# Pages of a folded weight: two single-page PSUM turns joined into one two-page turn

## The chip, the cores and the metric

The kernel runs on 1 core of one Trainium2 chip. The metric is the device time of one execution in microseconds; the number compared is the median of several executions. In 3 runs the kernel before took 734.44, 734.89 and 735.2 us, a median of 734.89 us.

## The reference, cut to what matters

An attention with 32 memory slots per head, followed by two feed-forward layers over all 2304 tokens:

```python
a = softmax(phi, axis=2)                       # over the sequence
k_m, v_m = a^T k, a^T v                        # per head: 32 x 64
attn = softmax(q @ k_m^T / 8)                  # per head: 576 x 32
x = (attn @ v_m) joined over the 8 heads       # 2304 x 512
x = relu(x @ w_in1)**2 @ w_out1                # layer 1, d_ff = 2048
h = x @ w_in2
out = (h * tanh(softplus(h))) @ w_out2         # layer 2
```

There are 4 batches, 8 heads, 576 tokens in a batch and a head size of 64. Everything is in 32-bit floats.

## The kernel before, in words

**What W' is.** The kernel never forms `attn @ v_m`. It folds the values into the first weight: for each batch b, W'_b = v_m(b) times w_in1, head by head, is 8 heads x 32 slots = 256 rows by 2048 columns, and layer 1 is then attn @ W'_b. W'_b is cut into 8 pages of 256 columns, named (b, j). To keep precision, a page holds a rounded high part and the low rest, and the product h (lines 713 to 715, `h_products`) takes three matmuls for each half of the 256 rows.

**A turn.** A page is made by 8 small matmuls (64 rows of the array, 32 columns of weights, 256 columns streamed) into the PSUM tile that `banks2` hands out: two banks, one buffer, tag "bb", shared with the attention scores and with the transposes of phi. ACT then copies the result to the high half of the page, and DVE subtracts the copy from the PSUM result to give the low half. Only then can the next user of "bb" start. `w_part` (line 580) does this for one page: matmuls at line 585, copy at 591, subtraction at 592. `w_pair` (line 605) does it for pages j and j + 1 of one batch: 16 matmuls at line 611, which put the first page into columns 0 to 255 and the second into columns 256 to 511 of both banks, and then the copies and subtractions of `take` (lines 618, 619) for the one and for the other. With `now=True` these are issued at once; otherwise they wait for the next step's `w_out`.

**The pages' places.** Pages live in a ring of 8 buffers (`page`, line 63); a new page takes the buffer of the one made eight earlier and waits for its last reader. The converted weights that the turns read, `wt["i1", j]`, lie in a ring of 4 buffers (line 229): page j + 4 of w_in1 can be written once both batches have used page j. The conversion `Conv` (from line 171) turns the raw 8-byte words into floats, one unit of 128 columns of w_in1 ("i1", u; page j is units 2j and 2j + 1) or one unit of w_out1 ("o1", u) for each `tick`: an ACT pass (line 204), two DVE passes (lines 234 and 240) and, for w_out1, a split (lines 223 and 263). `need(key, u)` ticks until that unit is done.

**The stages.** For batches 0 and 1, layer 1 goes in groups of d_ff blocks of 128: `GROUPS = [4, 6, 6]`, f = 0 to 3, 4 to 9, 10 to 15. The loop at line 1064 runs over 10 sub-tiles i. i = 0 to 3 are the first group, each on half a batch (288 tokens; i = 0 is written out by hand in `first_tile`). Then each of the other groups has three parts: part 0 is the first 344 tokens of batch 0, part 1 the remaining 232 of batch 0 with the first 232 of batch 1, part 2 the last 344 of batch 1 (i = 4 to 6 and i = 7 to 9). `a_tile` (line 724) runs one sub-tile: for each block fc it issues the product h, `tick(fc)`, relu and square, the split of the result g into high and low (lines 742 and 745), `mid(fc)`, the second product three blocks behind (`mm2_step`, lines 665 to 667, 12 matmuls), and last `post(fc)`, which is where the pages are made. The loads are SP's (sync) DMA queue's, issued by the conversion as its buffers come free.

**Where the pages are made before.** From `post` (line 1112): at i = 1, fc = 2 page (1,0) and fc = 3 page (1,1); at i = 3, fc = 2 page (0,2); at i = 4, fc = 4 page (0,3), fc = 6 page (0,4), fc = 8 page (1,2); at i = 5, fc = 4 the pair (1,3), (1,4); at i = 6, fc = 8 page (0,5); at i = 7, fc = 10 page (0,6), fc = 12 page (0,7), fc = 14 page (1,5); at i = 8, fc = 10 the pair (1,6), (1,7). The branch at lines 1114 to 1116 is never taken. Batches 2 and 3 get their pages in pairs.

**The order of the work.** The Python order is not the order on the chip: when the program is built, a scheduler with a timeline of its own puts each engine's instructions in order, and keeps to dependencies and to the explicit ones (`issue_after`, `written`). Matmuls of a page that nothing waits for yet can so land ahead of their place, or between others. Each engine then runs its own list strictly in that order.

After the ten sub-tiles, batches 2 and 3 follow as tiles of 288 tokens with all 16 blocks, beside the preparation of layer 2's weights (`Fold`), whose raw loads and stores share the DMA engines; then comes layer 2, whose order is fixed by hand.

Of the kernel before, what the change touches and what calls it, by code (L numbers as in the profile page):

```python
# [8 lines left out]
F32R = mybir.dt.float32r  # L9
# [7 lines left out]
B, H, S, D, M = 4, 8, 576, 64, 32  # L17
DM, FF = 512, 2048
P = 128
# [21 lines left out]
def body(tc, q, kvm, kvt, phi, w_in1, w_out1, w_in2, w_out2, out):  # L41
# [21 lines left out]
    def page(shape, dt, name):  # L63
        return PG.tile(shape, dt, tag="pg", name=name, bufs=NPG)
# [8 lines left out]
    for p in range(2):  # L73
        t = Y.tile([P, (NC + 1) * P], F32, name=f"phi{p}")
# [5 lines left out]
    def load_phi(b, p):  # L80
        nc.sync.dma_start(phi_t[p][:, at[p]:at[p] + S], phi[b, p])
# [14 lines left out]
    def load_q(b, half):  # L96

        q_t[b, half] = []
        for i in range(2):
            if b < 2 and half == 1:  # L100
                tag = f"wol{2 + i}" if b else f"wo{'hl'[i]}4"
                t = wo.tile([P, 2, T], F32, tag=tag, name=f"q{b}{half}{i}")
            else:
                t = Y.tile([P, 2, T], F32, tag="q", name=f"q{b}{half}{i}", bufs=2)
            nc.sync.dma_start(
                t.rearrange("p g t -> p (g t)"), q[b, half, :, 2 * i * T:2 * (i + 1) * T])
            q_t[b, half].append(t)
# [29 lines left out]
    wt = {}  # L137
# [15 lines left out]
    @contextlib.contextmanager  # L153
    def written(*engines):

        traced = nc.cur_bb.bb.instructions
        last = {x.engine: x for x in traced}
        seen = traced[-1]
        yield
        start = next(k for k in reversed(range(len(traced))) if traced[k] is seen) + 1  # L160
        for x in traced[start:]:
            if x.engine not in engines:
                continue
            if x.engine in last:
                tc.add_manual_dep(
                    x, last[x.engine].name,
                    mybir.DependencyInfo(mybir.DependencyClass.NoSync, mybir.DependencyReason.DATA),
                    reason="written")
            last[x.engine] = x
# [262 lines left out]
    def banks2(name):  # L432
        return psum2.tile([P, 2, 512], F32, tag="bb", name=name)

    rc_t, et_t, kk_t, kT, vT = {}, {}, {}, {}, {}
# [142 lines left out]
    wp = {}  # L578

    def w_part(b, j, lo, hi, split=False):  # L580

        ps = banks2(f"pw{b}{j}{lo}")[:, :, :hi - lo]
        for g in range(4):
            for p in range(2):
                nc.tensor.matmul(  # L585
                    ps[M * g:M * g + M, p], vT[b][D * p:D * p + D, M * g:M * g + M],
                    wt["i1", j][D * p:D * p + D, g, lo:hi], start=True, stop=True)
        if (b, j) not in wp:
            wp[b, j] = page([P, 2, 2, 256], F32R, f"wp{b}{j}")
        t = wp[b, j]  # L590
        nc.scalar.copy(t[:, 0, :, lo:hi], ps)
        rest = lambda: nc.vector.tensor_sub(t[:, 1, :, lo:hi], ps, t[:, 0, :, lo:hi].bitcast(F32))
        if split:
            return rest
        rest()
# [6 lines left out]
                f()  # L602
        wait_w.clear()

    def w_pair(b, j, now=False):

        ps = banks2(f"pw{b}{j}p")
        for i in range(2):
            for g in range(4):
                for p in range(2):  # L610
                    nc.tensor.matmul(
                        ps[M * g:M * g + M, p, 256 * i:256 * i + 256],
                        vT[b][D * p:D * p + D, M * g:M * g + M],
                        wt["i1", j + i][D * p:D * p + D, g], start=True, stop=True)

        def take(i):
            t = wp[b, j + i] = page([P, 2, 2, 256], F32R, f"wp{b}{j + i}")
            nc.scalar.copy(t[:, 0], ps[:, :, 256 * i:256 * i + 256])
            nc.vector.tensor_sub(t[:, 1], ps[:, :, 256 * i:256 * i + 256], t[:, 0].bitcast(F32))

        for i in range(2):
            if now:
                take(i)
            else:
                wait_w.append(lambda i=i: take(i))
# [25 lines left out]
    def drain(*lanes):  # L651
        while any(lanes):
            for lane in lanes:
                run_step(lane)
# [116 lines left out]
    def place(i):  # L771
        if i in deep:
# [3 lines left out]
    c1 = Conv(order, place,  # L776
              lambda key, u: key != "i1" or u < 8 or (1, u // 2 - 4) in wp)
# [257 lines left out]
    def attn_later(b, half):  # L1035
        def nxt():
            if b < 2:
                if (b, half) == (1, 0):
                    load_q(2, 0)
                return  # L1040
            nb, nh = (b, 1) if half == 0 else (b + 1, 0)
            if nb < B:
                load_q(nb, nh)
        return [[lazy(lambda: attn_unit(b, half, nxt)), 5 if b > 1 else 4]]
# [19 lines left out]
    for i, (f0, f1, segs) in enumerate(subs):  # L1064
        b, half, part = i // 2, i % 2, (i - 4) % 3 if i > 3 else None
        final = i == len(subs) - 1
        if i == 0:
            with written(mybir.EngineType.DVE, mybir.EngineType.Activation):
                first_tile()
            c1.hold = False  # L1070
            c1.store()
            c1.load(2 * GROUPS[0] - 3)
            continue
        elif i == 1:
            c1.limit, c1.after, c1.paced = 2 * GROUPS[0], "lo", True
            lanes, n_steps = [[iter(range(2)), 2]] + attn_later(1, 1), 1
        elif i == 2:
            c1.limit, c1.after = len(c1.order), (1, 0)
        elif i == 3:
            drain(lanes)  # L1080
            c1.after = (1, 1)
            load_q(2, 0)
            load_phi(2, 0)
            load_phi(2, 1)
            load_kv(2, 0)
            load_tail(2)
        elif i == 4:
            c1.after = None
        elif i == len(subs) - 2:
            lanes, n_steps = kv_later(2), 2  # L1090
        elif final:
            drain(lanes)
            lanes, n_steps = attn_later(2, 0), 2
            load_page(0)
            load_page(1)

        def tick(fc):
            if len(c1.done) < 2 * NF:
                c1.tick()
            else:  # L1100
                if not fold.loaded:
                    fold.load(3)
                if part and fc - f0 in (0, LAG + 1):
                    fold.tags = (("x", "at"), ("ys0", "x", "at"), ("ys0",), ("ys0", "ys1"))[
                        2 * part - 2 + (fc > f0)]
                if final or part == 1 and fc > f0:
                    fold.tick(pops=1)

        def mid(fc):
            run_step(lanes, n_steps)  # L1110

        def post(fc):
            if part is None:
                if half == 0 and fc % 2 == 0 and fc + 2 < f1 and i != 2:
                    c1.need("i1", fc + 3)
                    w_part(b, fc // 2 + 1, 0, 256)
                if i == 1 and fc + 1 == f1:
                    w_part(1, fc // 2, 0, 256)
                if half == 1 and fc + 2 == f1:
                    if b == 0:  # L1120
                        w_part(1, f0 // 2, 0, 256)
                    else:
                        c1.need("i1", f1 + 1)
                        w_part(0, f1 // 2, 0, 256)
            elif part == 0:
                if (fc - f0) % 2 == 0 and fc + 2 < f1:
                    c1.need("i1", fc + 3)
                    w_part(0, fc // 2 + 1, 0, 256)
                if fc >= f0 + 2:
                    c1.need("o1", fc - 2)  # L1130
                if fc + 1 == f1:
                    c1.need("o1", fc)
                if fc + 2 == f1:
                    w_part(1, f0 // 2, 0, 256)
            elif part == 1:
                if fc == f0:
                    w_pair(1, f0 // 2 + 1, True)
            elif fc + 2 == f1 and not final:
                c1.need("i1", f1 + 1)
                w_part(0, f1 // 2, 0, 256)  # L1140
            if final and fc - f0 in (1, 3):
                w_pair(2, fc - f0 - 1)
            if final and fc < f1 - 2:
                load_page(fc - f0 + 2)

        a_tile(segs, f0, f1, tick, mid, post, ("mm",) if i in (0, 1, 5) else ("mm", "b0"))
    drain(lanes)

# [8 lines left out]
    b, nb = 2, 3  # L1157
# [174 lines left out]
    now = 0  # L1332
# [139 lines left out]
    banks, tmp, g = {}, {}, {}  # L1472
# [4 lines left out]
    for now, (kind, i, one, two) in enumerate(plan):  # L1477
# [11 lines left out]
        if now + AHEAD < len(plan) and plan[now + AHEAD][0] == "b":  # L1489
            _, _, j, k = plan[now + AHEAD]  # L1490
# [73 lines left out]
```

## Time and profile before

| what | value |
|---|---|
| median of 3 runs | 734.89 us (734.44 to 735.2) |
| the profiled execution's own time | 734.3 us |
| its span, first to last instruction | 732.5 us |
| PE (matmuls) busy | 725.0 us, 99% |
| DVE busy | 523.5 us, 71% |
| ACT busy | 414.0 us, 57% |
| matmuls of single-page turns in the loop, line 585 | 10 turns x 16 records |
| matmuls of two-page turns, line 611 | 10 turns x 32 records |

The terms of the prediction are made against the profiled execution (734.3 us), which lies 0.59 us under the median. Each matmul of a fp32 turn shows as two records. In a timeline row the columns are the start in us, the length in us, the engine, the line, the operation, the output and inputs, the shape and the number of instructions merged into the row; in brackets stands how long the engine sat idle before it, and what ended that. Matmul lengths overlap: the time that one takes from PE is the distance between two starts.

### The profile page before, as it was taken

The numbers are of one execution on the slowest core, as the hardware profiler recorded it, in microseconds if no ns is written. First come the engines' busy times: TensorE is split into PE (matmuls) and PEld (weight loads), VectorE is DVE, ScalarE is ACT, GpSimd is POOL, SyncE is SP. The second block draws the span as 40 slices with busy tenths as digits, with TensorE's granted clock in tenths as the row PEclk, the third lists the DMA queues.
The fourth block names the chain that finished last, engine by engine and source line by source line (L and its number), as shares of the span: only waits on it lengthen the run. The fifth ranks groups of instructions, "written<-read, shape, count | busy, mean of one in ns | idle before, by whom it ended". The sixth has DMA issues, their size and how long they took to land.

```text
span 732.5 us, 15173 instructions
## 1 busy us (share of the span) xinstructions
PE 725.0 (99%) x5417; PEld 691.5 (94%) x5417; DVE 523.5 (71%) x1142; ACT 414.0 (57%) x937; POOL 62.0 (8%) x120
## 2 busy tenths in 40 slices
PE   8999999999999999999999999999999999999998
PEld 7788988998888899999999999999999999999997
DVE  5999766343887889899957769854658873556674
ACT  4869757553766698767644347532336551335552
POOL 0000000000122333243311000000000000000000
PEclk9999999999999999999999999999999999999999
DMA  9997542044689899878969998899988899888882
GB/s 337 400 407 280 178 136 92 30 159 151 229 303 377 305 316 339 287 274 312 330 230 358 392 315 250 271 298 305 307 251 249 253 293 297 250 252 249 254 272 77
DMA packets 88011, 195.26 MB, mean 267 GB/s; under 512 B 10112, under 2 KB 21376, under 8 KB 87936
## 3 DMA queue, kind: packets, MB, share of 16 engines
q1 hardware_dynamic: 78976, 164.92, 67.7%
q0 software_dynamic: 8960, 29.37, 10.3%
q8 instruction: 43, 0.70, 0.4%
q14 instruction: 32, 0.26, 0.1%
HBM read 151.26 MB, written 42.99 MB: 265 GB/s over the span
## 4 chain that ended last, share of the span: by engine, by line
PE 91%; DMA 4%; DVE 2%; ACT 2%; issue 1%; SPq 0%; DVEq 0%; ACTq 0%
PE a L667 8%; PE a L665 8%; PE a L666 8%; PE hb L1361 8%; PE hb L1363 8%; PE hb L1362 8%; PE h L713 5%; PE h L714 4%; PE h L715 4%; DMA raw_i<-in_moe_w_in_dram 2%; PE pw L585 1%; PE fill L789 1%; PE b22acc L1447 1%; PE b12acc L1445 1%; PE b02acc L1447 1%; PE b22acc L1445 1%
## 5 line engine op out<-in xcount | busy, mean ns | idle before, releaser
L665 PE MATMUL a<-g,o1h 128*128 128x288 f32 (+2 forms) x464 | 140.2, 311 | 1.3 <-ACT g L742 1.3
L666 PE MATMUL a<-g,o1l 128*128 128x288 f32 (+2 forms) x464 | 140.8, 309 | 0.0
L667 PE MATMUL a<-g,o1h 128*128 128x288 f32 (+2 forms) x464 | 127.9, 310 | 0.0
L1361 PE MATMUL hb<-ych,u 128*128 128x384 f32 x336 | 113.2, 337 | 0.0
L1362 PE MATMUL hb<-ycl,u 128*128 128x384 f32 x336 | 113.1, 336 | 0.0
L1363 PE MATMUL hb<-ych,u 128*128 128x384 f32 x336 | 113.0, 336 | 0.0
L1368 ACT ACTIVATE a<-hs 128x384 f32<-128x384 f32 x72 | 37.8, 526 | 117.9 <-DVE hs L1372 117.9
L665 PEld LDWEIGHTS a<-g,o1h 128*128 128x128 f32 x464 | 86.8, 188 | 5.5 <-ACT g L742 1.8
L736 ACT ACTIVATE s<-h 128x288 f32<-128x288 f32 (+2 forms) x112 | 49.1, 438 | 72.3 <-PE h L715 70.4
L666 PEld LDWEIGHTS a<-g,o1l 128*128 128x128 f32 x464 | 87.3, 188 | 2.1 <-issue 1.3
L667 PEld LDWEIGHTS a<-g,o1h 128*128 128x128 f32 x464 | 82.4, 188 | 2.9 <-DVE st L393 0.5
L1411 ACT CAST oph<-a 128x384 fp32r<-128x384 f32 x120 | 59.4, 512 | 37.9 <-PE b22acc L1447 7.4
L1412 DVE TENSOR_TENSOR opl<-a,oph 128x384 fp32r<-128x384 f32 x120 | 63.0, 554 | 22.5 <-ACT oph L1411 15.9
L713 PE MATMUL h<-ah,wp 128*128 128x288 f32 (+2 forms) x256 | 78.2, 306 | 0.4
L714 PE MATMUL h<-al,wp 128*128 128x288 f32 (+2 forms) x256 | 75.8, 296 | 0.2 <-DVE al L575 0.2
L715 PE MATMUL h<-ah,wp 128*128 128x288 f32 (+2 forms) x256 | 75.8, 297 | 0.0
L745 DVE TENSOR_TENSOR g<-s,g 128x288 fp32r<-128x288 f32 (+2 forms) x112 | 54.0, 484 | 22.2 <-ACT g L742 21.7
L1361 PEld LDWEIGHTS hb<-ych,u 128*128 128x128 f32 x336 | 63.0, 188 | 0.3 <-DVE hu L1383 0.3
L1363 PEld LDWEIGHTS hb<-ych,u 128*128 128x128 f32 x336 | 63.0, 188 | 0.0
L1362 PEld LDWEIGHTS hb<-ycl,u 128*128 128x128 f32 x336 | 63.0, 188 | 0.0
L1372 DVE TENSOR_TENSOR hs<-hu,hb 128x384 f32<-128x384 f32 x72 | 39.7, 553 | 25.9 <-PE hb L1363 24.1
L713 PEld LDWEIGHTS h<-ah,wp 128*128 128x128 f32 x256 | 48.1, 188 | 9.4 <-issue 4.1
(322 smaller groups left out, 1529.0 us busy)
## 6 DMA issues: line engine op xcount, KB each, us to landing
u<-wf_i SPq DMA_DIRECT2D x168, 256.0 KB, 4.0
u<-wf_o SPq DMA_DIRECT2D x168, 256.0 KB, 3.2
raw_i<-in_moe_w_in_dram SPq DMA_DIRECT2D x32, 512.0 KB, 5.7
raw_o<-in_moe_w_out_dram SPq DMA_DIRECT2D x32, 512.0 KB, 6.3
wf_i<-st POOLq DMA_DIRECT2D x56, 256.0 KB, 5.2
wf_o<-st POOLq DMA_DIRECT2D x56, 256.0 KB, 4.9
win1r<-w_i SPq DMA_DIRECT2D x16, 512.0 KB, 5.3
kv<-in_kvm_dram SPq DMA_DIRECT2D x5, 1024.0 KB, 7.4
```

The costliest lines, as they stand in the source:

```text
L665: nc.tensor.matmul(o, wh[:, c, cs], sh, start=first, stop=False)
L666: nc.tensor.matmul(o, wl[:, c, cs], sh, start=False, stop=False)
L667: nc.tensor.matmul(o, wh[:, c, cs], sl, start=False, stop=last)
L713: nc.tensor.matmul(ph, w[:, 0, hg, fs], hi[:, hg], start=(hg == 0), stop=False)
L714: nc.tensor.matmul(ph, w[:, 0, hg, fs], lo[:, hg], start=False, stop=False)
L715: nc.tensor.matmul(ph, w[:, 1, hg, fs], hi[:, hg], start=False, stop=(hg == 1))
L745: marks["lo"] = nc.vector.tensor_sub(sl, s, sh.bitcast(F32))
L1361: nc.tensor.matmul(ps, wh, yh[:, d], start=(j < 4 and d == 0), stop=False, **kw)
L1362: nc.tensor.matmul(ps, wh, yl[:, d], start=False, stop=False, **kw)
L1363: nc.tensor.matmul(ps, wl, yh[:, d], start=False, stop=end, **kw)
L1411: marks["hi"] = nc.scalar.copy(hi, x)
L1412: marks["lo"] = sub(lo, x, hi.bitcast(F32))
```

## The change

`w_pair` gets an argument `across`: with it, the two pages of a turn are page j of batch b and page j of batch b + 1. All ten `w_part` calls of `post` become five `w_pair` calls with `now=True`.

```diff
-    def w_pair(b, j, now=False):
+    def w_pair(b, j, now=False, across=False):
         ps = banks2(f"pw{b}{j}p")
-        for i in range(2):
+        two = [(b, j), (b + 1, j) if across else (b, j + 1)]
+        for i, (bb, jj) in enumerate(two):
             for g in range(4):
                 for p in range(2):
                     nc.tensor.matmul(
                         ps[M * g:M * g + M, p, 256 * i:256 * i + 256],
-                        vT[b][D * p:D * p + D, M * g:M * g + M],
-                        wt["i1", j + i][D * p:D * p + D, g], start=True, stop=True)
+                        vT[bb][D * p:D * p + D, M * g:M * g + M],
+                        wt["i1", jj][D * p:D * p + D, g], start=True, stop=True)
         def take(i):
-            t = wp[b, j + i] = page([P, 2, 2, 256], F32R, f"wp{b}{j + i}")
+            t = wp[two[i]] = page([P, 2, 2, 256], F32R, "wp%d%d" % two[i])
...
-                if i == 1 and fc + 1 == f1:
-                    w_part(1, fc // 2, 0, 256)
                 if half == 1 and fc + 2 == f1:
                     if b == 0:
-                        w_part(1, f0 // 2, 0, 256)
+                        w_pair(1, f0 // 2, True)
                     else:
                         c1.need("i1", f1 + 1)
-                        w_part(0, f1 // 2, 0, 256)
+                        w_pair(0, f1 // 2, True, True)
             elif part == 0:
-                if (fc - f0) % 2 == 0 and fc + 2 < f1:
-                    c1.need("i1", fc + 3)
-                    w_part(0, fc // 2 + 1, 0, 256)
+                if fc == f0:
+                    c1.need("i1", fc + 5)
+                    w_pair(0, fc // 2 + 1, True)
...
-                if fc + 2 == f1:
-                    w_part(1, f0 // 2, 0, 256)
             elif part == 1:
                 if fc == f0:
                     w_pair(1, f0 // 2 + 1, True)
             elif fc + 2 == f1 and not final:
                 c1.need("i1", f1 + 1)
-                w_part(0, f1 // 2, 0, 256)
+                w_pair(0, f1 // 2, True, True)
```

The five turns after, named A to E from here on:

- A, at i = 1, fc = 2: pages (1,0) and (1,1)
- B, at i = 3, fc = 2: pages (0,2) and (1,2), a joint turn of both batches
- C, at i = 4, fc = 4: pages (0,3) and (0,4), after units up to i1 9
- D, at i = 6, fc = 8: pages (0,5) and (1,5), a joint turn
- E, at i = 7, fc = 10: pages (0,6) and (0,7), after units up to i1 15

The never-taken branch goes too. Nothing is computed otherwise than before.

## Rows read from the trace of the kernel before

**Rows 1.** The page, part 1: busy us, share of the span, instructions of each engine.
```profile
PE 725.0 (99%) x5417; PEld 691.5 (94%) x5417; DVE 523.5 (71%) x1142; ACT 414.0 (57%) x937; POOL 62.0 (8%) x120
```

**Rows 2.** Waits of PE over the whole span: us in total, times, longest us.
```profile
PE a L665 <- ACT g L742: 1.3, 2, 0.9
```

**Rows 3.** Timeline of PE around a whole single-page turn.
```profile
49.70 0.29 PE L666 MATMUL a<-g,o1l 128*128 128x288 f32 x1
49.83 0.29 PE L667 MATMUL a<-g,o1h 128*128 128x288 f32 x1
50.06 0.66 PE L585 MATMUL pw<-win,vT 64*32 64x256 f32 x16
...
50.89 0.29 PE L666 MATMUL a<-g,o1l 128*128 128x288 f32 x1
```

**Rows 4.** Timeline of PE around a two-page turn, pages (1,3) and (1,4).
```profile
91.02 0.32 PE L667 MATMUL a<-g,o1h 128*128 128x344 f32 x1
91.27 1.09 PE L611 MATMUL pw13p<-win,vT 64*32 64x256 f32 x32
...
92.56 0.27 PE L713 MATMUL h<-ah,wp 128*128 128x232 f32 x1
```

**Rows 5.** Timeline of PE: pieces of cut turns, of (0,5), (1,5) and batch 3.
```profile
108.84 0.63 PE L585 MATMUL pw<-win,vT 64*32 64x256 f32 x6
...
147.29 0.32 PE L667 MATMUL a<-g,o1h 128*128 128x344 f32 x1
147.54 0.64 PE L585 MATMUL pw<-win,vT 64*32 64x256 f32 x10
...
148.38 0.32 PE L714 MATMUL h<-al,wp 128*128 128x344 f32 x1
...
252.00 0.62 PE L611 MATMUL pw30p<-win1r,vT 64*32 64x256 f32 x2
```

**Rows 6.** Busy time in stretches of 20 us: PE, PEld, DVE, ACT, POOL, clock, DMA share, GB/s.
```profile
60.00:80.00 20.00, 19.93 (x164) 18.35 (x163) 19.59 (x45) 19.96 (x50) 0.00 (x0) 1.00 0.73 255
...
100.00:120.00 20.00, 20.00 (x137) 16.68 (x136) 8.57 (x14) 10.46 (x21) 0.00 (x0) 1.00 0.33 106
...
220.00:240.00 20.00, 19.09 (x229) 17.53 (x227) 14.85 (x36) 14.56 (x37) 6.16 (x11) 1.00 0.98 373
```

**Rows 7.** Timeline of ACT and of DVE: evacuation of the two-page turn of rows 4.
```profile
93.18 0.58 ACT L618 CAST wp<-pw13p 128x512 fp32r<-128x512 f32 x1
94.78 0.59 ACT L618 CAST wp<-pw13p 128x512 fp32r<-128x512 f32 x1 [1.01 <-DVE wp L619]
...
94.06 0.68 DVE L619 TENSOR_TENSOR wp<-pw13p,wp 128x512 fp32r<-128x512 f32 x1
95.39 0.69 DVE L619 TENSOR_TENSOR wp<-pw13p,wp 128x512 fp32r<-128x512 f32 x1 [0.65 <-ACT wp L618]
```

**Rows 8.** Line 618: ACT's idle time before all 20 copies, in us and times.
```profile
  DVE wp L619: 2.3, 3
```

**Rows 9.** Timelines of ACT and DVE: evacuation of the turns that start at 50.06 and 57.05 us.
```profile
50.83 0.59 ACT L591 CAST wp<-pw 128x512 fp32r<-128x512 f32 x1 [2.95 <-PE pw L585]
...
60.30 0.56 ACT L591 CAST wp<-pw 128x512 fp32r<-128x512 f32 x1
...
63.67 0.69 DVE L592 TENSOR_TENSOR wp<-pw,wp 128x512 fp32r<-128x512 f32 x1
```

**Rows 10.** Timelines of DVE and PE: unit i1 9 done, and block 6 of sub-tile 4.
```profile
72.44 0.68 DVE L240 SCALAR_TENSOR_TENSOR win<-raw_i,win 128x512 int32<-128x512 int32 x1
...
75.33 0.32 PE L713 MATMUL h<-ah,wp 128*128 128x344 f32 x1
...
75.65 0.32 PE L715 MATMUL h<-ah,wp 128*128 128x344 f32 x1
```

**Rows 11.** Timeline of DVE: first conversion pass of unit i1 12.
```profile
85.65 0.43 DVE L234 TENSOR_SCALAR win<-raw_i 128x512 int32<-128x512 int32 x1 [3.19 <-PE pw L585]
```

**Rows 12.** Chain of work that ended last: start us, length us, what.
```profile
226.92 9.05 DMA raw_i<-in_moe_w_in_dram
```

## The prediction

> **What bounds the kernel now.** I read the page first: PE is busy 725.0 us, 99% of the span of 732.5 [rows 1]. Next the waits of PE over the whole span: the largest is 1.3 us in two pieces, at 217 and 238 us [rows 2], far behind the change, and between 40 and 160 us, where all the turns concerned lie, that view names no wait of PE at all. So where the change acts PE's own issue rate bounds, and what a turn costs is the time that it takes from the stream of full-size matmuls. That is read in the timeline, as the distance between starts less the usual step of the neighbours.
>
> A whole single-page turn: from the start at 49.83 to the one at 50.89 is 1.06 us [rows 3]; two of these 288-column matmuls step 0.13 each, so the turn took 1.06 - 0.26 = 0.80; with unrounded starts I get 0.79. A two-page turn: 91.02 to 92.56 is 1.54 [rows 4], less two steps of 344 columns at 0.16 (75.33 to 75.65 holds two of them [rows 10]) is 1.22. Two pages singly take 1.58, jointly 1.22. The difference is a fixed part of about 0.36 a turn: PE's gap before the first small matmul (49.83 to 50.06, where 0.13 is usual) and after the last.
>
> The second view that matters is the work beside PE. From 60 to 80 us ACT is busy 19.96 and DVE 19.59 of 20 us; from 100 to 120 they are busy 10.46 and 8.57 [rows 6]. In the first of these stretches PE only just outruns them.
>
> **Part by part.**
>
> 1. *Fewer turns.* Ten pages leave the single-page turns. Eight were whole, 8 x 0.79 = 6.32 us. Two, (0,5) and (1,5), were cut in two pieces by the scheduler: 6 and 10 records each [rows 5]. A piece costs nearly a whole turn: 147.29 to 148.38 is 1.09, less two steps of 344 (0.32), 0.77; the four pieces 3.05. Before: 9.37. After, five whole two-page turns: 5 x 1.22 = 6.10. The number of matmuls stays, and all of the 9.37 is PE time with nothing beside it to hide it. Term: **-3.27 us**.
>
> 2. *Pieces after.* The new turns are filler until a page is due, and longer. Among the turns before, 2 of 10 single and 1 of 10 double ones were cut. The cut (0,5) was made ahead of its place, from the gap at 108.84 on, and D, which is made at that same place and twice as long, has the same reason to be cut. I take one cut: a piece more costs 2 x 0.77 less 0.79, **+0.75**. Bounds: none (0) and three more pieces (+2.2), as one double turn of batch 3 was cut into four, the last with 2 records [rows 5].
>
> 3. *Evacuation of B and C.* Copies and subtractions stay ten each, with the same shapes. Their order changes: in a two-page turn the second copy waits for the first subtraction, and the second subtraction for that copy. ACT stood idle 1.01 us and DVE 0.65 us in this way [rows 7]. Over all 20 copies of the double turns, however, ACT waited so only 3 times, 2.3 us together [rows 8]: where it has other work queued, the wait is filled. A lies at 50 us, where ACT had just idled 2.95 us [rows 9]; D and E lie past 100 us, with time to spare [rows 6]. B and C lie in the full stretch. B brings page (1,2) from 85 [rows 11] to about 57 us [rows 9]: by 80 us one page more than before has been evacuated, a copy of about 0.58 and a subtraction of 0.69. PE runs up to three blocks ahead of the second product, which covers some of it. Between nothing and one full idle wait for each of B and C (2 x 1.01), I take **+0.2**, near the lower end, because of those 3 times in 20. As a gain I allow 0.3, two steps of a 288-column matmul, since A makes page (1,1) earlier than its first reader comes.
>
> The Trainium skill, page "PSUM — Partial Sum Buffer", section "PSUM bank collisions raise a hardware error", says that no two engines may be in one bank and quadrant at once, two reads included, and that they have to be kept apart by bank. Both pages of a double turn share both banks, so by it pairing always serialises the evacuation, and the sum would have +2.0 in place of +0.2; the trace shows that serial order [rows 7], and that it seldom costs ACT time [rows 8].
>
> 4. *The earlier need.* C wants unit i1 9 two blocks sooner. By the loop's count of ticks i1 9 is started in that very block's `tick`, so `need` adds one tick: some ACT and DVE passes come one block (2.8 us) earlier, none is added. Their raw words are in the chip: no load is behind it. Before, i1 9 was done at 73.1 us, and the first matmul that reads page (0,3) started at 75.33, the first that reads its low half at 75.65 [rows 10]. With no advance at all, C would run 73.2 to 74.2, and a prompt copy, subtraction included, would end at about 75.6. **0**, with 0 to 1.5 us as bounds. SP issues the later raw loads and the stores of w_in1 in the same order, a little sooner; no load is added.
>
> 5. *The rings.* The page ring hands (0,7) the buffer of (1,2), last read at block 5 of sub-tile 6, well before (0,7) is due; all other takeovers are of pages long dead. Unit i1 12 may overwrite page 2 of w_in1 already after B: DVE's wait of 3.19 us at 85.65 [rows 11] goes, but PE did not wait there: 0.
>
> 6. *What follows.* After 160 us nothing is changed. PE's two waits there [rows 2] hang on ACT, behind raw loads of which the longest on the chain took 9.05 us [rows 12], at a DMA share of 0.98 [rows 6]. Those loads are issued by the kernel's own progress, so the stage should move as a whole: 0. A slightly other order could shift them by up to about 1 us either way.
>
> Sum: -3.27 + 0.75 + 0.2 = -2.3 us. Against the profiled execution 734.3 - 2.3 = 732.0; that run stands 0.59 under the median, so the median comes to **732.6 us**. What a measurement of this kernel can tell from no change is about 0.2%, 1.47 us: under 733.4 is faster, over 736.4 slower.
>
> **The rivals.**
>
> *Cut turns.* The scheduler fills its gaps with halves of the longer turns: three or four cuts give +2.2 to +2.9 in place of 0.75, 734.1 to 734.8. For it: the cut turns and the four pieces in batch 3 [rows 5]; against: nine of ten double turns whole. Chance 0.12.
>
> *Serial evacuation in the full stretch.* B and C stop ACT for 1.01 us each, nothing fills it, and PE waits as long: -3.27 + 0.75 + 2.0, 734.4. For it: the full ACT [rows 6]; against it: 17 of 20 copies without such a wait [rows 8]. Chance 0.10.
>
> *Late loads give it back.* PE comes to 217 us sooner but the loads do not; the two waits grow by most of 2.3 us: 734 to 734.9. Against it: what issues them is the work that itself comes sooner. Chance 0.05.
>
> *Page (0,3) comes too late: slower.* Before, that page had a turn of its own two blocks ahead of need; now it waits for i1 9 and shares C. If the evacuation drags in the full queues as that of the turn at 57.05 did, whose subtraction began at 63.67 and ended at 64.36 [rows 9], 7.3 us behind, the page is there at 73.2 + 7.3 = 80.5, against a need at 75.65: PE waits 4.9 us where little else is left to do, 734.9 - 3.27 + 0.75 + 4.9 = 737.3. It decides from about 79.6 us on (75.65 + 2.5 saved + 1.47). Against it: the page at 57 was not due for 11 us, and an urgent one would be put first. Chance 0.10.
>
> *No cut at all, the small waits go too:* -3.27 - 0.3, 731.3. Chance 0.06.
>
> **How the numbers follow.** The sum as it stands has 0.57. Faster: 0.57 + 0.06 = 0.63. Same: 0.12 + 0.10 + 0.05 = 0.27. Slower: 0.10. The range runs from 731.0 (no cut, small waits gone, 0.3 of shift behind) to 735.0, which takes in the three cases of no change; left out are the late page and small tails, under 2 in 10.
>
> **What would show it.** Right: five turns of 32 records at line 611 before 160 us, none at line 585 after 27 us, each taking 1.22 us between its neighbours; the stages from sub-tile 4 on ever earlier, by about 0.3, 0.7, 1.0 and then 2 to 3 us by 150 us, and the same lead at 240 us and at the end. Pieces under 32 records show cuts. Wrong: a wait of PE on `wp` at block 6 of sub-tile 4, near 75 us; larger waits on `g` near 217 and 238 us; or a changed order of the second products that makes PE wait between 57 and 80 us.

## The result, and the profile after

The kernel after took **743.89 us** in the median of 6 runs (739.96 to 746.65), the kernel before on the same chip 734.66 (6 runs). The ratio is 1.0110, 95% interval 1.0092 to 1.0128: slower by 1.1%, where 0.3% faster was forecast. The profiled execution took 745.09 us, its span 743.3; that is 10.8 us more than before.

The page, part 1 (busy us, share of the span, instructions), against [rows 1], and the waits of PE, against [rows 2]:

```profile
PE 732.0 (98%) x5417; PEld 695.5 (94%) x5417; DVE 523.4 (70%) x1142; ACT 413.7 (56%) x937; POOL 61.8 (8%) x120
```

```profile
PE a L666 <- ACT g L743: 4.7, 2, 3.5
...
PE h L716 <- DVE wp L620: 0.2, 1, 0.2
```

Two things are to be seen. PE is *busy* 7.0 us longer with the same 5417 instructions, although five turns were taken away; and the wait on ACT's g (line 743, 742 before) grew from 1.3 to 4.7 us, 3.5 of it in one piece. (Lines of the kernel after stand one higher than before from 608 to the end of the loop over sub-tiles.)

**Where in the span.** I compare the start of the same piece of work in both traces. The start-up differs from trace to trace, so every difference is taken from the matmul of the product h that waits for `al` early on (36.51 us before, 37.20 after; in the traces of the experiments below it starts between 36.73 and 38.20). Then the kernel after stands at +3.48 us where the pair (2,0),(2,1) is made (186 us before), +3.02 at the pair (2,2) (199 us), +10.16 at the pair (3,0) (247 us), and +10.15 at the last matmul. So 3 us are lost where the change acts, 7 us between the pairs (2,2) and (3,0), where nothing was changed, and none after that.

**The first part: turns in pieces.** The timeline of PE, matmuls of line 612, with one neighbour where a cost is read; a whole turn has 32 records. A (pw10p), B (pw02p), C (pw03p), the old pair (pw13p), D (pw05p), E (pw06p), and far behind the change the pair (2,4) (pw24p):

```profile
50.52 0.29 PE L668 MATMUL a<-g,o1h 128*128 128x288 f32 x1
50.74 1.09 PE L612 MATMUL pw10p<-win,vT 64*32 64x256 f32 x32
51.77 0.40 PE L666 MATMUL a<-g,o1h 128*128 128x288 f32 x1
52.01 0.29 PE L667 MATMUL a<-g,o1l 128*128 128x288 f32 x1
...
57.48 1.05 PE L612 MATMUL pw02p<-win,vT 64*32 64x256 f32 x20
...
59.72 0.62 PE L612 MATMUL pw02p<-win,vT 64*32 64x256 f32 x4
...
61.00 0.62 PE L612 MATMUL pw02p<-win,vT 64*32 64x256 f32 x2
...
61.88 0.62 PE L612 MATMUL pw02p<-win,vT 64*32 64x256 f32 x4
...
65.14 0.62 PE L612 MATMUL pw02p<-win,vT 64*32 64x256 f32 x2
...
75.69 0.65 PE L612 MATMUL pw03p<-win,vT 64*32 64x256 f32 x12
...
77.00 0.62 PE L612 MATMUL pw03p<-win,vT 64*32 64x256 f32 x4
...
78.42 0.66 PE L612 MATMUL pw03p<-win,vT 64*32 64x256 f32 x16
...
87.37 0.64 PE L612 MATMUL pw13p<-win,vT 64*32 64x256 f32 x10
...
89.09 0.63 PE L612 MATMUL pw13p<-win,vT 64*32 64x256 f32 x6
...
95.88 0.66 PE L612 MATMUL pw13p<-win,vT 64*32 64x256 f32 x16
...
105.90 0.37 PE L667 MATMUL a<-g,o1l 128*128 128x464 f32 x1
106.20 0.62 PE L612 MATMUL pw05p<-win,vT 64*32 64x256 f32 x2
106.75 0.48 PE L666 MATMUL a<-g,o1h 128*128 128x464 f32 x1
107.06 0.37 PE L667 MATMUL a<-g,o1l 128*128 128x464 f32 x1
107.27 0.37 PE L668 MATMUL a<-g,o1h 128*128 128x464 f32 x1
...
113.78 0.64 PE L612 MATMUL pw05p<-win,vT 64*32 64x256 f32 x10
...
118.41 0.66 PE L612 MATMUL pw05p<-win,vT 64*32 64x256 f32 x16
...
123.11 0.62 PE L612 MATMUL pw05p<-win,vT 64*32 64x256 f32 x4
...
131.51 1.09 PE L612 MATMUL pw06p<-win,vT 64*32 64x256 f32 x32
...
212.84 0.65 PE L612 MATMUL pw24p<-win1r,vT 64*32 64x256 f32 x12
214.41 1.05 PE L612 MATMUL pw24p<-win1r,vT 64*32 64x256 f32 x20
```

A and E are whole: from 50.52 to 52.01 is 1.49 us, less two steps of 0.13, 1.22 with unrounded starts, as in [rows 4]. B is in 5 pieces, C in 3, D in 4 (x2, x10, x16, x4), and the pair (1,3),(1,4), one turn before [rows 4], is now in 3. What a piece costs is read at 106.20: from 105.90 to 107.06 is 1.16, less two steps of 464 columns (107.06 to 107.27: 0.21), 0.74 us. That is for one of the 16 matmuls, and nearly as much as a whole single turn of 8 (0.79). The lengths of the rows say why: 2 records take 0.62 us, 16 take 0.66, and only what goes beyond 16 takes more (20 records 1.05, 32 records 1.09). The eight matmuls of a page run side by side, so one of them alone takes as long as all eight; only about 0.36 us of a piece (2 x 0.79 less 1.22) is the fixed part. Summed in this way, the turns A to E and the pair take 14.28 us in 17 pieces; before, the same pages took 10.58 in 13 (9.36 for the ten single turns, 1.22 for the pair): **+3.7 us**, where -2.5 was forecast. The pair (2,4), whole before, costs 0.74 more (1.96 in two pieces, 1.22 before).

**The second part: a load behind two others.** The timeline of SP's queue where batch 2 hands over to batch 3, of the kernel before and of the one after (start us, length of the issue, line, what is loaded):

```profile
223.70 0.38 SPq L86 DMA_DIRECT2D kv<-in_kvm_dram  x1
224.55 0.33 SPq L1061 DMA_DIRECT2D win1r<-w_i  x1
226.92 0.33 SPq L319 DMA_DIRECT2D raw_i<-in_moe_w_in_dram  x1
227.34 0.45 SPq L1061 DMA_DIRECT2D win1r<-w_i  x1
```

```profile
229.28 0.38 SPq L86 DMA_DIRECT2D kv<-in_kvm_dram  x1
230.13 0.85 SPq L1062 DMA_DIRECT2D win1r<-w_i  x2
231.92 2.25 SPq L319 DMA_DIRECT2D raw_i<-in_moe_w_in_dram  x2
```

Before, the raw load of unit 8 of layer 2's w_in ("i2" 8) went out between the loads of pages 2 and 3 of w_in1; after, behind both. The chain of work shows what that does to it, against [rows 12]:

```profile
231.92 13.29 DMA raw_i<-in_moe_w_in_dram
```

13.29 us in place of 9.05. ACT and then PE, in their timelines, stand behind it:

```profile
239.85 0.45 ACT L738 ACTIVATE s<-s 128x288 f32<-128x288 f32 x1
245.24 0.65 ACT L339 ACTIVATE raw_i<-raw_i 128x512 f32<-128x512 f32 x1 [4.94 <-DMA raw_i<-in_moe_w_in_dram]
245.79 0.41 ACT L743 CAST g<-s 128x288 fp32r<-128x288 f32 x1
```

```profile
246.26 0.61 PE L666 MATMUL a<-g,o1h 128*128 128x288 f32 x1 [3.55 <-ACT g L743]
246.67 0.44 PE L667 MATMUL a<-g,o1l 128*128 128x288 f32 x1
246.91 0.44 PE L666 MATMUL a<-g,o1h 128*128 128x288 f32 x1
```

ACT's next instruction after 239.85 is the pass over that raw unit; it stands idle 4.94 us, and the copy of g that PE needs is queued behind the pass. PE stops for 3.55 us. And when it goes on, a 288-column matmul steps 0.24 us, where 0.13 is the step of [rows 3]: TensorE's clock has fallen. Busy time in stretches shows it (us, PE, PEld, DVE, ACT, POOL, granted clock, DMA share, GB/s):

```profile
245.00:252.00 7.00, 5.74 (x24) 5.72 (x25) 3.66 (x10) 3.57 (x10) 1.07 (x2) 0.53 0.50 163
252.00:260.00 8.00, 8.00 (x81) 6.21 (x80) 6.63 (x16) 4.68 (x14) 1.61 (x3) 0.98 0.81 273
```

A mean of 0.53 from 245 to 252 and 0.98 behind it is the lower level (1.2 GHz) from about 245.4 to 252.3. PE had the work to fill it from 246.26: 6.0 us at 0.24 a step in place of 0.13, some 2.7 us lost. In the trace before the clock is full throughout.

**The sum of the profiled execution:** turns +3.7, pair (2,4) +0.7, PE's two waits on g +3.4 (1.33 and 3.71 between starts, less a usual step; before 0.62 and 1.02), clock +2.7, together +10.5 against a measured +10.15. The other 0.4 came back in small places that I did not follow up.

Of the six executions of this kernel, two had a mean granted clock of 1.000 (739.96 and 740.83 us); the four others, at 0.995 to 0.997, took 743.53 to 746.65. They lie 3.1 to 6.3 us above the middle of those two, and the clock cost 2.7 in the profiled one, so something besides the clock differs as well; only one execution was profiled, and what it is stays open. With no fall of the clock the kernel is still some 5.7 us slower than before.

### The profile page after: what moved, and what is told of

It is laid out like the page before. It is cut to its first block, busy times and chain, and to the rows that moved or that the text cites. A ratio compares the mean times of both kernels' runs of the same rounds, so it can differ in the third digit from the quotient of the medians.

```text
span 743.3 us, 15179 instructions
## 1 busy us (share of the span) xinstructions
PE 732.0 (98%) x5417; PEld 695.5 (94%) x5417; DVE 523.4 (70%) x1142; ACT 413.7 (56%) x937; POOL 61.8 (8%) x120
## 4 chain that ended last, share of the span: by engine, by line
PE 90%; DVE 4%; DMA 3%; ACT 1%; issue 1%; POOL 0%; ACTq 0%; DVEq 0%; POOLq 0%
PE a L666 8%; PE a L668 8%; PE hb L1358 8%; PE a L667 8%; PE hb L1360 8%; PE hb L1359 8%; PE h L714 4%; PE h L716 4%; PE h L715 4%; DMA raw_i<-in_moe_w_in_dram 3%; PE fill L790 1%; PE b02acc L1442 1%; PE b22acc L1442 1%; PE b12acc L1442 1%; PE b02acc L1444 1%; PE b03acc L1443 1%
## 5 line engine op out<-in xcount | busy, mean ns | idle before, releaser
L666 PE MATMUL a<-g,o1h 128*128 128x288 f32 (+2 forms) x464 | 142.2, 314 | 4.7 <-ACT g L743 4.7
L668 PE MATMUL a<-g,o1h 128*128 128x288 f32 (+2 forms) x464 | 129.6, 311 | 0.0
```

The costliest lines, as they stand in the source:

```text
L666: nc.tensor.matmul(o, wh[:, c, cs], sh, start=first, stop=False)
L668: nc.tensor.matmul(o, wh[:, c, cs], sl, start=False, stop=last)
```

## The experiments

Two explanations stood against each other at the start: that the cut turns are the loss, or that the order of SP's loads is, with the wait and the clock behind it. There are ten runs of eight kernels on three chips (w_hp2 and b_hps2 are w_hp and b_hps again). "Net end" is the start of the last matmul against the kernel before, each less its own start-up as above; it is from one profiled execution and leaves the start-up out.

| kernel | median us (runs) | before, same chip | ratio [95%] | net end, us |
|---|---|---|---|---|
| after | 743.89 (6) | 734.66 | 1.0110 [1.0092, 1.0128] | +10.15 |
| a_sp | 739.08 (4) | 735.0 | 1.0048 [1.0029, 1.0068] | +6.16 |
| b_hp | 738.86 (4) | 735.0 | 1.0049 [1.0032, 1.0067] | +3.74 |
| s_ADE | 739.18 (8) | 735.48 | 1.0047 [1.0033, 1.0062] | +4.30 |
| b_hps | 734.3 (12) | 735.48 | 0.9985 [0.9973, 0.9997] | -0.54 |
| b_hps2 | 734.58 (12) | 735.6 | 0.9989 [0.9976, 1.0001] | -1.06 |
| w_hp | 733.94 (12) | 735.0 | 0.9989 [0.9977, 1.0001] | -2.40 |
| w_hp2 | 734.44 (12) | 735.6 | 0.9983 [0.9970, 0.9995] | -2.70 |
| w_all | 737.91 (12) | 735.48 | 1.0026 [1.0009, 1.0042] | +1.73 |
| w_k | 734.49 (12) | 735.6 | 0.9984 [0.9969, 0.9999] | -1.04 |
| w_k30 | 732.84 (6) | 735.6 | 0.9959 [0.9945, 0.9972] | -2.73 |

### a_sp: the kernel after, with the raw load put back ahead

```diff
-                load_page(j)
+                with behind(fold.sent, ("i2", 8) if j > 1 else None):
+                    load_page(j)
```

(`fold.sent` keeps the DMA that `Fold.load` issues for each unit.)

> The changed kernel with one edit: the last two of the four page loads issued at the end of the first tile of batch 2 are put behind the raw load of unit i2 8 in SP's queue; the turns, with all their pieces, stay as they are. Theory (SP's new order delays that raw load, ACT waits for it, PE waits 3.7 us at 246 us and then runs 6.8 us at half clock): the raw load lands within about 10 us in place of 13.3, the wait falls to about 1 us, no half clock, 743.9 - 2.7 - 3.3 = about 738 us. Rival (the wait comes from the cut turns, which bring PE late to a stretch of full DMA engines, and not from the order of the loads): the wait stays 3 us or more, the half clock too, 741 to 746 us.

739.08 us, 4.8 less than the kernel after. Between the two traces this raw load is the only one of SP's 520 transfers that stands at another place in the queue. It took 8.04 us instead of 13.29, and the wait at 246 us is gone. What is left of the loss stands in two other places: the turns are cut as in the kernel after (at the pair (2,0) it stands at +3.44, the kernel after at +3.48), and the earlier of the two waits on g is now the longer. PE's timeline there, and the stretch behind it:

```profile
223.88 0.40 PE L667 MATMUL a<-g,o1h 128*128 128x288 f32 x1 [2.18 <-ACT g L744]
```

```profile
224.00:228.50 4.50, 4.50 (x24) 4.48 (x25) 4.16 (x10) 2.91 (x8) 0.88 (x3) 0.62 0.90 277
```

After that wait too the clock fell, for 3.4 us, which was not expected. So the order of two loads is worth about 5 us, and the rest is in the pieces and what they make late.

### w_hp: the kernel after, with whole turns

```diff
-        for i, (bb, jj) in enumerate(two):
+        with (tc.high_priority() if now else contextlib.nullcontext()):
+            for i, (bb, jj) in reversed(list(enumerate(two))):
...
```

The scheduler takes the 16 matmuls of each turn of batches 0 and 1 as urgent, the later page first, so that nothing is put between them.

> The changed kernel with the 16 matmuls of each turn that is made at once given precedence when the program is ordered, and the page that is ready last put first, so that no other matmul comes between; the raw load of unit i2 8 stands ahead of the page loads again. Theory (the prediction's sum was right for whole turns, and the loss is pieces and the late loads): turns A to E and the pair (1,3) take 1.22 us each, about 7.3 us where the kernel before took 10.6; late waits as before (1.6 us) and one cut more in batch 2 (0.7): about 732 us. Rival (two-page turns crowd ACT and DVE near 60 to 80 us): PE waits on pages or on g there, 734 to 737 us.

733.94 us. A, B, C, E and the pair (1,3) each take 1.22 us, D 1.48, of which 0.26 is a wait for the PSUM buffer, until DVE's subtraction for the turn before (line 621) ends. At the pair (2,0) the kernel stands at -3.05 us: **that is the first term of the forecast, -3.27, nearly whole**, although D's wait and one of 0.25 on page (1,1) are in it. About 732 us was expected. The rival's number, 734, came closer, but not its mechanism: the view of waits names none of PE on a page or on g between 60 and 80 us. In the profiled execution (733.54) the net end is 2.40 us ahead, and 1.69 of that is lost in the start-up, where `al` came at 38.20 us in place of 36.51; in w_all, with the same turns, it came at 36.73. With whole turns the raw load was also issued ahead of kv and the two pages, by the scheduler alone, so this run by itself does not separate the two causes.

### b_hp and b_hps: single turns as before, made whole

b_hp puts the 8 matmuls of each `w_part` turn under `tc.high_priority()` in the kernel before, and changes nothing else:

```diff
-        for g in range(4):
+        with (contextlib.nullcontext() if split else tc.high_priority()):
+            for g in range(4):
...
```

> The kernel before, single-page turns kept, their 8 matmuls given precedence, so that (0,5) and (1,5) are whole; by this the order of SP's loads becomes the one of the changed kernel, both page loads ahead of the raw load of unit i2 8. Theory that this order makes the late wait: turns 1.5 us less, one more cut in batch 2 (+0.7), but a wait of 3 us or more near 238 us, and half clock after it if it is that long: 737 to 741 us. Rival (the late wait follows from late turns): 733 to 735 us, wait about 1 us.

738.86 us, 4 us slower than before, although no turn of batches 0 and 1 is in pieces and it stands at -1.28 at the pair (2,0). SP's queue shows both page loads ahead of the raw load, as in the kernel after, and the chain of work and PE's waits show the rest:

```profile
224.64 1.51 SPq L1062 DMA_DIRECT2D win1r<-w_i  x2
226.96 2.26 SPq L319 DMA_DIRECT2D raw_i<-in_moe_w_in_dram  x2
```

```profile
226.96 12.61 DMA raw_i<-in_moe_w_in_dram
```

```profile
PE a L666 <- ACT g L743: 4.2, 2, 3.4
```

Behind the long wait the clock was at the lower level for 3.4 us. This kernel has nothing of the change in it, no turn shared by two batches and no two-page turn that was not there before. Whether the order of the queue is what makes it slower, b_hps says: it adds to it the edit of a_sp.

> b_hp (single turns unbroken) with one edit more: the loads of pages 2 and 3 of the next batch stand behind the raw load of unit 8 on the queue of SP. Theory: the raw load is back to 8 to 9 us, the 3.55 us wait and the half clock go, and the time falls by about 4.5 us to 734 us (735.0, less two joined turns at 0.75 each, plus 0.75 for the pair 24 that is cut, and up to 0.7 of waits on ACT). Against w_hp (same order of loads, pages two in a turn) it is then the price of single turns alone: 5 times 2 x 0.79 less 5 times 1.22, 1.8 us more than w_hp. Rival (the order of loads is not what cost b_hp its 4 us): it stays at 738 to 739 us.

734.3 us. Its queue and the raw load on the chain:

```profile
226.41 0.33 SPq L320 DMA_DIRECT2D raw_i<-in_moe_w_in_dram  x1
226.83 2.79 SPq L1063 DMA_DIRECT2D win1r<-w_i  x2
```

```profile
226.41 9.55 DMA raw_i<-in_moe_w_in_dram
```

9.55 us, a wait on g of 0.9 in place of 3.55, full clock, 4.6 us less in the median. Between b_hp and b_hps only the order of three loads differs: of SP's 520 transfers the raw load alone stands at another place. So that order makes b_hp slower. In the landings, too, the order of issue is kept: in b_hp kv 232.38, pages 234.72 and 237.06, raw 239.57; in b_hps kv 233.63, raw 235.97, pages 238.31 and 239.85. Each half megabyte lands 1.5 to 2.5 us behind the one ahead of it, and with two pages ahead of it the raw load landed 3.6 us later. The Trainium skill, page "DMA: Bandwidth & Descriptors", section "Queues, rings and completion order", says that on each engine descriptors are taken in the order of the ring; these landings agree.

### s_ADE: half of the change

B and C undone, A, D and E kept:

```diff
-                        w_pair(0, f1 // 2, True, True)
+                        w_part(0, f1 // 2, 0, 256)
...
-                if fc == f0:
+                if i in [7] and fc == f0:
                     c1.need("i1", fc + 5)
                     w_pair(0, fc // 2 + 1, True)
+                if i not in [7] and (fc - f0) % 2 == 0 and fc + 2 < f1:
+                    c1.need("i1", fc + 3)
+                    w_part(0, fc // 2 + 1, 0, 256)
...
+                if i in [4] and fc + 2 == f1:
+                    w_part(1, f0 // 2, 0, 256)
```

> The kernel after, with B and C undone: only the joint turns A and D and the turn E (0,6),(0,7) read two pages; (0,2), (1,2), (0,3), (0,4) and the others are single turns as before, and with these the pair of 13 goes back to one unbroken turn. In program order PE is cut less often than in the kernel after, but the queue of SP still issues both window loads and the kv load ahead of the raw load of unit 8. Theory (the queue's order is the larger part of the loss): a PE wait of 3 to 4 us on ACT's g near the end of batch 1, half clock after it, 738 to 741 us. Rival (the cut turns are the loss): two cut turns less than the kernel after, about 733.5 us.

739.18 us, as the theory said: the rival's 733.5 is out. Up to the pair (2,0) this kernel is 1.18 us *ahead* of the one before, with D in three pieces; then both page loads stand ahead of the raw load (13.56 us on the chain), PE waits 3.86 us between starts at 241.59, the clock falls, and at the pair (3,0) it is 4.39 behind. In the stretch before 200 us, then, this half of the change was a gain; it was lost in the queue.

### w_all and w_k: every pair whole

w_all gives high priority to all pairs (`with tc.high_priority():`).

> w_hp with high priority for every pair's matmuls, those of 13, 24 and the last batch too. Theory: the pair 24 becomes whole again (0.75 us less than w_hp's 1.96), the raw load stays ahead of the page loads, no half clock: 732 to 733.3 us, below both kernels. Rival: the moved instructions bring back a wait of PE on ACT's g near 220 or 246 us and with it half clock: 735 us or more.

737.91 us, the rival's side, but not by its mechanism. D waited 1.21 us for the PSUM buffer, and this time SP issued the raw load first, then the two pages, then kv, and the load that came too late was kv. PE's timeline:

```profile
239.13 1.08 PE L488 MATMUL pk<-kv,et 128*32 128x128 f32 x32 [3.52 <-DMA kv<-in_kvm_dram]
```

w_k keeps the loads of pages 2 and 3 behind kv as well:

```diff
+                with behind(fold.sent, ("i2", 8) if j > 1 else None):
+                    with behind(kv_sent, max(kv_sent) if j > 1 else None):
+                        load_page(j)
```

> w_all (all pairs whole) with the loads of pages 2 and 3 behind both the raw load of unit 8 and the kv load on SP's queue; w_all lost 3.5 us waiting for that kv load, which stood behind the two page loads. Theory: the kv wait falls from 3.5 us to under 1, and the kernel ends 2 to 3.5 us before w_all: 734 to 736 us by the runs, below w_hp if no other wait grows. Rival (kv is late for another reason, the raw load that still stands ahead of it): the wait stays and the time too, 737 to 738.

734.49 us, 3.4 less than w_all, as expected; the longest wait for kv is 0.9 in place of 3.5. Again it is the two page loads, needed late, that must not stand ahead of a load that is needed soon. Below w_hp it did not come: D now waits 1.5 us for the PSUM buffer.

### w_hp2 and b_hps2: what two pages in a turn are worth

w_hp and b_hps again, side by side on one chip; both have whole turns in batches 0 and 1 and the raw load ahead of the page loads. Their queues are not the same beyond that: five of SP's 520 transfers stand at other places, and the raw load is ahead of kv in w_hp2 and behind it in b_hps2.

> w_hp again, to stand beside b_hps on one chip: pages two in a turn, every turn whole, the raw load of unit 8 ahead of the page loads. In the traces, less the start (first wait on DVE's al at 38.20 in w_hp and 36.97 in b_hps), w_hp ended 1.9 us earlier than b_hps. Theory (two pages in a whole turn save 0.36 us a pair, 1.8 us in five pairs): 1.5 to 2 us below the second b_hps. Rival (what the turns save is given back in the time, as the two ratios to the kernel before, 0.9989 and 0.9985, say): no difference.

> b_hps again, beside the second w_hp on one chip: pages one in a turn, every turn whole, the same order of loads. Theory: 1.5 to 2 us above the second w_hp, 0.5 to 1.2 us below the kernel before. Rival: the same time as the second w_hp.

In the traces w_hp2 is 1.47 us ahead of b_hps2 at the pair (2,0) and 1.64 at the end (w_hp against b_hps: 1.75 and 1.86); the forecast's unit price, 0.36 us for each pair, five times, is 1.8. A turn and the joint turn D in PE's timeline of w_hp2:

```profile
74.94 0.29 PE L668 MATMUL a<-g,o1l 128*128 128x288 f32 x1
75.16 1.09 PE L613 MATMUL pw03p<-win,vT 64*32 64x256 f32 x32
76.19 0.80 PE L669 MATMUL a<-g,o1h 128*128 128x288 f32 x4
...
92.16 1.10 PE L613 MATMUL pw05p<-win,vT 64*32 64x256 f32 x32 [0.48 <-DVE wp L621]
```

The times do not bear it out: medians 734.44 and 734.58, ratios 0.9983 and 0.9989 with overlapping intervals, in the first pair of runs 0.9989 and 0.9985. Among the executions at full granted clock alone the two-page kernel is ahead by 0.5 us both times (733.88 and 734.39; 733.61 and 734.17). Executions with a mean of 0.997 or 0.998 are 4 of 12 in w_hp2 and 3 of 12 in w_hp, and 2 of 12 in each of the single-page runs. Part of the traces' lead is lost in the start-up, which the net end leaves out: it is 0.31 us longer in w_hp2 than in b_hps2 and 1.23 longer in w_hp than in b_hps, so that the spans differ by 1.3 and 0.6. Whole single turns with the loads in this order give about 1 us; that two pages in a turn add to it in the median is not shown, with 0.14 us between the medians side by side. Where the rest of the traces' 1.6 goes stays open.

### w_k30: a version below both kernels

w_hp with the loads ordered as in w_k, and high priority for the pair (3,0) too, which is in four pieces in the kernel before [rows 5]:

```diff
-        with (tc.high_priority() if now else contextlib.nullcontext()):
+        with (tc.high_priority() if now or (b, j) == (3, 0) else contextlib.nullcontext()):
```

> w_hp, the loads of pages 2 and 3 behind raw unit 8 and kv, and high priority for the pair 30 too, which is in three pieces in w_hp (four in the kernel before, 3.03 us). Theory: the pair 30 in one turn saves 1.1 us against w_hp: about 0.9975 of the kernel before. Rival: an earlier pair 30 takes the place of matmuls that covered the wait on ACT's g near 257, which grows: no gain over w_hp.

**732.84 us, 0.9959 [0.9945, 0.9972] of the kernel before**, and all six executions at full clock. The pair (3,0), in PE's timeline:

```profile
248.12 1.09 PE L615 MATMUL pw30p<-win1r,vT 64*32 64x256 f32 x32
```

It beats both; 0.9975 was expected. In the profiled execution it stands at -2.73, no further than w_hp2: its waits on ACT at 217 and 219 us (1.04 and 1.47 between starts; 0.98 and 0.35 in w_hp2) took what the pair gave. In the runs it lies 1.6 us below w_hp2, 1.0 below w_hp2's runs at full clock. The order of the loads has no part in that: all 520 transfers of SP stand in the same order in the traces of w_hp2 and w_k30. The pair, 1.22 us in place of 2.30 in three pieces, would give 1.1, but the one trace does not show it at the end.

## Why the prediction was wrong, point by point

**Part 1, fewer turns (-3.27): right as a price.** 1.22 us for a whole two-page turn (A at 50.74, E at 131.51, and in w_hp all but the wait of D) and 0.79 for a whole single one held to the hundredth, and with whole turns the lead at the pair (2,0) was 3.05 and 2.73 us. The Trainium skill, page "TensorEngine Tiling (Array Packing)", section "Tiling Modes", says that a change of tiling mode drains the TensorE; the fixed part of a turn, 0.36 us, agrees.

**Part 2, pieces after (+0.75, bounds 0 and +2.2): this step failed first.** It counted one cut. There were nine in A to E, and two more in the pair (1,3),(1,4), which I took to stay as it was [rows 4]: 14.28 us where whole turns make 7.32 (6 x 1.22), so +7.0 in place of +0.75; and the pair (2,4) was cut far behind the change. What misled me was the count of cuts among the turns before, 3 of 20, taken as a rate for the turns after. The scheduler puts matmuls whose page is not due yet into its gaps, a few at a time [rows 5]; I read B, C and D as such matmuls, since each of them makes a page earlier than before. That this is the scheduler's reason was not tried; that high priority keeps all of them whole was (w_hp). The rival "cut turns" had the mechanism, but ended at four cuts; with the cuts as they came, 734.3 + 3.7 + 0.7, it would have said about 739.

**Part 6, what follows (0, up to 1 us either way): this step failed next, and cost nearly as much, 3.4 us of waits and 2.7 of clock.** "Those loads are issued by the kernel's own progress, so the stage should move as a whole." It did not move as a whole: the order in which SP issues them came out otherwise. Part 4 said it too ("SP issues the later raw loads and the stores of w_in1 in the same order, a little sooner"). The order is the scheduler's, and other turns in batches 0 and 1 were enough for it to put two page loads ahead of a raw load. b_hp shows that this comes with no two-page turn at all, b_hps that it costs 4.6 us. A DMA share of 0.98 [rows 6] and a 9.05 us load on the chain [rows 12] were reason to ask what becomes of that load when others step ahead of it. The forecast should have held a rival in which an order changes, not only one in which loads are late. Of its own signs of being wrong, "larger waits on `g` near 217 and 238 us" is the one that came.

**The clock: not in the forecast at all.** Before, the longest wait behind the start-up was 0.9 us [rows 2], and the clock was full. After, it cost 2.7 us in the profiled execution; the executions at 0.997 and at 0.995 are 3.5 and 5.5 us above those at full clock (743.89 and 745.87 against 740.39), which is more than the clock's own price.

**Part 3, evacuation (+0.2).** Over all pairs ACT stood idle for the subtraction 3.6 us in 4 pieces (line 619), against 2.3 in 3 [rows 8]. PE saw 0.25 us of it, the longer step at 55.95 on page (1,1). The +2.0 that the prediction gives for two full idle waits did not come.

**Part 4 and the slower rival, page (0,3) too late.** The result was slower, but not by this: the view of waits has no wait on `wp` there, even with C in three pieces until 79. ACT's copy of that page starts at 79.2, so its first reader, at 75.33 before [rows 10], came over 4 us later, and PE had other work in its place. **Part 5, the rings:** no wait there, as said. **"Late loads give it back"** came nearest to the second loss in place (217 to 247 us), but its mechanism, a lead that the loads do not follow, is another: there was no lead.

## What to carry to other kernels

Where a scheduler orders the engines, a bundle of small matmuls is cheap only as long as it stays whole: if its result is not urgent, it may be used as filler, and a piece of one matmul costs nearly what the eight of a page cost (0.74 and 0.79 us here), so bind it together or count the pieces. And a change in one stage can turn the order of a DMA queue in another: where the DMA share is near 1, pin the loads that an engine's strict order waits for ahead of those that are needed later, and look at the queue of the changed kernel before believing that the stages behind "move as a whole".

## What was not expected of the hardware

- TensorE's clock fell to its lower level around a single stop in a busy stretch. In the kernel after, with a wait of PE of 3.71 us between starts, it was low for 6.8 us, from 0.8 us before the wait ended. With waits of 3.55 (b_hp), 3.86 (s_ADE) and even 2.34 us (a_sp) it was low for 3.4 us, from 0.1 to 1.2 us after the end of the wait. In the trace of w_all it did not fall with a wait of 3.68 us. But seven of w_all's twelve executions have a mean clock of 0.995 or 0.997, and two of the six of the kernel after have 1.000. So it falls in some executions of a kernel and not in others, and the length of the wait alone does not tell; what does is open.
- The half-megabyte load in the full stretch took 13.29, 13.56 and 12.61 us behind kv and two pages (after, s_ADE, b_hp), 9.05 behind kv and one page (before), and 9.55, 8.04 and 7.73 behind kv alone (b_hps, a_sp, b_hps2). Two pages ahead of it cost 3 to 6 us; that one page does is not shown.
- Single executions of one and the same kernel differ by 4 to 6 us (w_hp2: 732.35 to 736.72; w_k: 732.37 to 738.39). Part of it goes with the granted clock: in w_hp2 the median is 733.88 at 1.000 and 735.87 at 0.998. Not all of it does: the slowest execution of w_k had 1.000.
